# An mLSTM cell and a mixture of depths on one core: output gates loaded and used later, the routed layers one step later

## The chip, the cores and the metric

The kernel runs on one core of a Trainium2 chip. The metric is the device time of one execution in microseconds. A profiled execution also gives a span, from the first to the last instruction of the program; the time lies a little above the span.

Five engines work beside each other, each through its own list of instructions in order: TensorE (PE), VectorE (DVE), ScalarE (ACT), GpSimd (POOL) and SyncE (SP). SP only issues transfers here. All transfers run on the core's 16 DMA engines.

## The reference

Two blocks follow each other. The first is an mLSTM cell for 4 batches, 8 heads, 768 positions and a head dimension of 40:

```
m_new  = maximum(f[t] + m, i[t]);  f_stab = exp(f[t] + m - m_new);  i_stab = exp(i[t] - m_new)
C = f_stab * C + i_stab * outer(v[t], k[t])
n = f_stab * n + i_stab * k[t]
y[t] = sigmoid(o[t]) * (C @ q[t]) / maximum(abs(n @ q[t]), 1)
```

Its result, with the heads side by side, is x of 4 x 768 rows of 320 numbers. The second block works on each batch of x:

```
scores = x[b] @ w_gate
top_idx = the 128 rows of x[b] with the highest scores
out[b] = x[b];  out[b, top_idx] += sigmoid(scores[top_idx]) * (relu(x[b, top_idx] @ w1) @ w2)
```

w1 is 320 x 1024, w2 is 1024 x 320. Everything is float32.

## The kernel before, in words

**Steps.** The work is cut into 12 steps n = 0 to 11: batch b = n // 3, positions 256 (n % 3) to 256 (n % 3) + 255. A step handles all 8 heads, in chunks of 64 positions. The order of all instructions is written out by hand: each engine runs its instructions in the order in which the program text issues them, and a wait holds all that is behind it on the same engine.

**Loads.** SP issues them. `load(n)` brings v, k and q of a step (320 KB each, in two halves for v and k), `load_o(n)` the output gates o (320 KB, two halves). The table `queue` says at which step's text a load is issued; since SP does little else, only its order in SP's list counts, and the buffer it fills: `k_t`, `q_t`, `v_t` and `o_t` have four buffers each, so `load(n)` must wait until step n - 4's data has been used, and `load_o(n)` until `sigmoid(n - 4)` has run.

**One ordinary step n.** PE makes the scores (`scores`, L300), DVE masks them (`masked`, L306). PE turns the next step's k (`turn` with "kT", L232, ACT copies the result, L234), ACT spreads out the next step's q (`widen`, L216), PE makes the next step's update of the state (`update`, L267, from k and the weighed values wv), and DVE adds it up (`states`, L279 to L287). PE reads the states for this step (`read`, L322), turns the next q ("qT", L232), and adds the part inside the chunks (`attend`, L332). DVE divides (`divide`, L341 to L346), which gives y. POOL weighs the values of step n + 2 (`weigh`, L244). ACT makes the sigmoid of the output gates (`sigmoid`, four instructions, L250), POOL multiplies y by it into x (`output`, L354) and issues the two transfers that store x (`store`, L361). DVE makes the scores of the router from x (`router`, L369). `fill` (L221) issues matmuls whose result nobody reads; the third argument of `turn` counts them.

**The routed block of a batch b.** Once all six groups of 128 scores of a batch are there, `spread` (L405) puts them across all partitions through PE and ACT (L412), `ranks` counts for each row how many are greater, half on DVE (L418), half by signs on ACT (L423), and `select` (L472) makes a table of the chosen. `numbers` (L517) turns it into row numbers. `fetch` (L523) is an indirect transfer on POOL that gathers the chosen rows from the output in DRAM, so it comes behind the stores of that batch; `fetched` (L533, L535) turns them, `layer1` (L560 to L566) and `layer2` (L576) are the two layers, `weighed` (L585) scales the result, and `add` (L589) is an indirect transfer on POOL that adds it to the output in DRAM. The program orders an `add` behind earlier transfers that read or write the same range of output rows, and the other way round; POOL stands until those have landed.

**Where these stand.** Batch 0: spread in step 3, ranks in step 4, fetch in step 6. Step 8 is not an ordinary step: the function `layers(8)` replaces it after its scores. It holds the layers of batches 0 and 1, the outputs of steps 6, 7 and 8 (which steps 6 and 7 leave out), the two adds, and the preparation of step 9. Batch 1's spread stands in step 7, its ranks inside `layers`. Batch 2: spread and ranks at the end of `layers`, numbers and fetch in step 9, layers in step 11. Batch 3 comes at the end.

**PSUM.** The pool `ps_u` has one buffer of two banks, which `update`, the first half of `layer1` and others take in turn; `ps_s` (scores, spread) and `ps_h` (read) have one, `ps_t` (turn and smaller tiles) two.

Of the kernel before, what the change touches and what calls it, by code (L numbers as in the profile page):

```python
# [9 lines left out]
FP = mybir.dt.float32  # L10
# [16 lines left out]
def _fast(ctx, tc, q, k, v, i_gate, f_gate, o_gate, w_gate, w1_in, w2_in, out):  # L27
# [6 lines left out]
    NS = S // 256  # L34
    N = B * NS
# [10 lines left out]
    ps_u = ctx.enter_context(tc.tile_pool(name="ps_u", bufs=1, space=PSUM))  # L46
# [55 lines left out]
    load_kv(0, v_t, v)  # L102
    load(1)
    wg = const.tile([128, DM], FP, name="wg")
    load_o(0)
    load(2)
    load_o(1)
    ident = const.tile([128, 128], FP, name="ident")

    def zero(t):  # L110
# [136 lines left out]
    def sigmoid(n):  # L247
        for r in range(2):
            for c in range(2):
                ACT.activation(out=so_t[n % 3][64 * c:64 * c + 64, r], in_=o_t[n % NO][64 * r:64 * r + 64, c], func=AF.Sigmoid)  # L250
# [98 lines left out]
    def output(n):  # L349
        b, s = divmod(n, NS)  # L350
        for r in range(2):
            x, o = x_t[b % 2][:, 2 * s + r, 0:DM], so_t[n % 3][:, r].rearrange("s h d -> s (h d)")
            order = "s (p j d) -> s j p d"
            POOL.tensor_tensor(out=x.rearrange(order, j=2, d=D), in0=pending[n]["y"][:, r].rearrange("s (j p) d -> s j p d", j=2),  # L354
                               in1=o.rearrange(order, j=2, d=D), op=OP.mult)

    def store(n):
        b, s = divmod(n, NS)
        for c in range(2):
            a = 256 * s + 128 * c  # L360
            (POOL if n < N - 1 else SP).dma_start(out=out[b, a:a + 128, :].rearrange("(r t) d -> t r d", t=64),  # L361
                          in_=x_t[b % 2][64 * c:64 * c + 64, 2 * s:2 * s + 2, 0:DM])

    def router(n):
        b, s = divmod(n, NS)
        x = x_t[b % 2][:, 2 * s:2 * s + 2]
        scr = work.tile([128, DM], FP, name="scr", bufs=1)
        for r in range(2):
            DVE.tensor_tensor_reduce(out=scr, in0=x[:, r, 0:DM], in1=wg, scale=1.0, scalar=0.0,  # L369
                                     op0=OP.mult, op1=OP.add, accum_out=x[:, r, DM:DM + 1])  # L370
        del pending[n]
# [18 lines left out]
    dep = {}  # L390
# [6 lines left out]
    def spread(b, r0, r1, pool=None, copied=True):  # L397

        x, w = x_t[b % 2], r1 - r0
        if pool is None:  # L400
            pB = ps_s.tile([128, 2, 512], FP, name="pB", tag="s")
        else:
            pB = pool.tile([128, 2, 512], FP, name="pB", tag="h")
        for r in range(w):
            PE.transpose(pB[:, r // 4, 128 * (r % 4):128 * (r % 4) + 128],  # L405
                         x[:, r0 + r, DM:DM + 1].to_broadcast([128, 128]), ident)
        return spread_copy(pB, w) if copied else pB

    def spread_copy(pB, w):
        flat = pB.rearrange("p j t -> p (j t)")[:, 0:128 * w]  # L410
        sb = mod.tile([128, 128 * w], FP, name=f"sb{w}", bufs=1)
        ACT.copy(out=sb, in_=flat)  # L412
        return sb
# [206 lines left out]
    def weights2():  # L620
        for h in range(2):
            SP.dma_start(out=w2[:, 4 * h:4 * h + 4], in_=w2_in[512 * h:512 * h + 512].rearrange("(f p) d -> p f d", p=128))

    queue = {0: (load, 3, load_o, 2), 1: (load, 4, load_o, 3, load, 5, load_o, 4), 2: (load, 6, load_o, 5),
             4: (load, 7, load, 8, weights1, None, load_o, 6), 5: (load_o, 7, weights2, None, load_o, 8), 6: (load, 9),
             7: (load, 10), 9: (load_o, 9, load_o, 10, load, 11, load_o, 11)}

    def layers(n):

        fetched(0)  # L630
        read(n)
        ranks(1)
        select(1)
        attend(n)
        layer1(0, 0)
        numbers(1, ps_t.tile([128, 3], FP, name="pi", tag="t"))
        fetch(1)
        sigmoid(n - 2)
        output(n - 2)
        store(n - 2)  # L640
        layer1(0, 4)
        divide(n)
        valued(0)
        sigmoid(n - 1)
        output(n - 1)
        store(n - 1)
        layer2(0)
        router(n - 2)
        router(n - 1)
        fetched(1)  # L650
        weighed(0)
        sigmoid(n)
        output(n)
        store(n)
        valued(1)
        layer1(1, 0)
        router(n)
        layer1(1, 4)
        weigh(n + 1)
        add(0)  # L660
        turn(n + 1, "kT")
        widen(n + 1)
        pB = spread(2, 0, 2 * NS, ps_h, False)
        turn(n + 1, "qT")
        dep[2] = {"sb": spread_copy(pB, 2 * NS)}
        ranks(2)
        layer2(1)
        weighed(1)
        select(2)
        weigh(n + 2)  # L670
        update(n + 1)
        states(n + 1)
        add(1)

    for n in range(N):
        b, s = divmod(n, NS)
        more = n + 1 < N
        todo = queue.get(n, ())
        for act, i in zip(todo[0::2], todo[1::2]):
            act(*(() if i is None else (i,)))  # L680
        scores(n)
        masked(n)
        if n == 8:
            layers(n)
            continue
        if n == 0:
            update(0)
            states(0)
        if n in (3, 6, 11):
            router(n - 1)  # L690
        if n == 4:
            ranks(0)
            select(0)
        if more:
            turn(n + 1, "kT", (0, 2, 6, 2, 2, 4)[n] if n < 6 else 0)
            widen(n + 1)
        if 0 < n and more:
            update(n + 1)
            if n != 9:
                states(n + 1)  # L700
            if n not in (3, 6, 7, 9):
                router(n - 1)
        if not more:
            sigmoid(n)
            gated(n)
            fill(ps_t.tile([128, 128], FP, name="pf", tag="t"), 2)
        read(n)
        if n == 9:
            numbers(2, ps_s.tile([128, 2, 512], FP, name="pi", tag="s")[:, 0, 0:3])
            states(n + 1)  # L710
        if n + 2 < N and n != 7:
            weigh(n + 2)
        if n == 6:
            fetch(0)
        if n == 0:
            update(1)
            states(1)
        if more:
            turn(n + 1, "qT")
            if n in (3, 7):  # L720
                dep[n // 4] = {"sb": spread(n // 4, 0, 2 * NS)}
            if n not in (6, 7):
                sigmoid(n)
        else:
            fetched(b - 1, 2)
            dep[b] = {"sb4": spread(b, 0, 4)}
            layer1(b - 1, 0)
            valued(b - 1)
            ranks_first(b)
        attend(n)  # L730
        divide(n)
        if n == 4:
            numbers(0, spare(n + 1)[:, 1, 0:3])
        if n == 9:
            fetch(2)
        if more and n not in (6, 7):
            output(n)
            store(n)
        if n == 0:
            POOL.memset(k_t[3][:, :, :, D:DP], 0.0)  # L740
            tables()
        if n == 1:
            margins()
# [376 lines left out]
```

## Time and profile before

| what | value |
|---|---|
| time, median of 3 runs | 163.75 us (161.92 to 165.38) |
| the profiled execution: time | 163.37 us |
| the profiled execution: span | 161.3 us |
| granted TensorE clock, mean | 0.989 |
| busy: PE, DVE, ACT, POOL | 144.5, 95.2, 89.0, 84.5 us |
| moved by DMA | 24.31 MB, of which 18.75 MB through SP's queue and 4.92 MB through POOL's |

How to read it: a matmul in float32 shows as two records on PE, and weight loads (PEld) overlap matmuls. In the lists below a row has the start and the length in microseconds, the engine ("q" after it: its queue, which issues transfers), the line of the kernel, the operation, what it writes and reads, the shape and the count; in brackets stands how long the engine was idle before it, and what ended that. A row of a group (it begins with the line) ends with the busy time, the mean nanoseconds of one instruction, and the idle time before. A row of transfers ends with the kilobytes of one, if they are known, and the median microseconds from issue to landing. A row with three numbers between strokes gives the shortest, the median and the longest instruction in nanoseconds.

### The profile page before, as it was taken

To read this page: it belongs to the slowest core of one execution; us is meant where nothing else is said; L and a number is where in the kernel's file an instruction comes from. 1 tells how busy PE (TensorE), PEld (TensorE's weight loads), DVE (VectorE), ACT (ScalarE), POOL (GpSimd) and SP (SyncE) were. 2 spreads that over 40 slices of the span, in tenths; PEclk is the share of its full clock that TensorE was granted. 3 is DMA by queue.
4 is the path that set the end of the run, shared out by engine and by line. 5 is a ranking of instruction groups with operands and counts; after the bars stand their busy time and mean duration, and the time that the engine had idled before them with its cause. 6 is when DMAs were issued, how large, how long until landed. Compare 5 with 4: busy or idle time off the path is not lost.

```text
span 161.3 us, 6676 instructions
## 1 busy us (share of the span) xinstructions
PE 144.5 (90%) x2864; PEld 125.4 (78%) x2864; DVE 95.2 (59%) x251; ACT 89.0 (55%) x179; POOL 84.5 (52%) x114
## 2 busy tenths in 40 slices
PE   7989899998998998899989989799999999999900
PEld 7779789997987987799878779579888897898500
DVE  6478384656769957594596542197776959411000
ACT  1667396566598747425475675874648669213000
POOL 7137278988575492892004969847480924212020
PEclk9999999999999999999999999999999999999995
DMA  4999899999979989999989999999513210330110
GB/s 88 198 163 196 137 169 205 188 186 205 194 169 227 187 161 208 175 262 296 157 240 232 206 266 172 216 190 184 100 45 87 46 39 4 81 41 0 53 51 2
DMA packets 91880, 24.31 MB, mean 151 GB/s; under 512 B 88097, under 2 KB 90466, under 8 KB 91842
## 3 DMA queue, kind: packets, MB, share of 16 engines
q1 hardware_dynamic: 89920, 18.75, 65.1%
q0 software_dynamic: 1728, 4.92, 11.0%
q8 instruction: 24, 0.39, 1.1%
q10 hardware_dynamic: 194, 0.13, 0.3%
q14 instruction: 14, 0.11, 0.2%
HBM read 19.20 MB, written 4.59 MB: 147 GB/s over the span
## 4 chain that ended last, share of the span: by engine, by line
PE 63%; DMA 14%; ACT 7%; issue 5%; DVE 5%; ACTq 1%; POOL 1%; DVEq 0%; POOLq 0%
PE pt L232 10%; DMA k<-in_k_dram 9%; PE pU L267 9%; PE py L576 8%; PE pH L332 7%; PE pH L322 6%; PE pU L560 6%; PE pS L300 4%; PE ph L560 2%; DMA i_sb<-in_i_gate_dram 2%; PE pU L564 2%; DMA xe<-out_dram,idx 2%; PE pX L498 2%; ACT sgn L423 1%; PE pt L221 1%
## 5 line engine op out<-in xcount | busy, mean ns | idle before, releaser
L244 POOL TENSOR_TENSOR wv<-v,cols 64x656 f32<-64x656 f32 x23 | 30.1, 1312 | 25.0 <-DMA v<-in_v_dram 14.1
L354 POOL TENSOR_TENSOR x<-y,so 128x320 f32<-128x320 f32 x24 | 21.1, 896 | 10.9 <-DVE y L346 4.2
L236 ACT COPY qT<-pt 128x512 f32<-128x512 f32 x24 | 13.8, 635 | 17.2 <-PE pt L232 17.2
L250 ACT ACTIVATE so<-o 64x320 f32<-64x320 f32 x48 | 22.4, 467 | 0.9
L234 ACT COPY kT<-pt 128x512 f32<-128x512 f32 x24 | 13.3, 587 | 15.0 <-PE pt L232 15.0
L369 DVE CUSTOM_DVE_ANT_0 scr<-x,wg 128x320 f32<-128x320 f32 x22 | 13.8, 628 | 8.1 <-POOL x L354 6.5
L576 PE MATMUL py<-w,hT 128*128 128x320 f32 x64 | 18.2, 437 | 0.3 <-ACT qT L236 0.3
L279 DVE TENSOR_TENSOR C<-pU,C 128x164 f32<-128x164 f32 x40 | 13.1, 327 | 7.0 <-PE pU L267 5.9
L267 PE MATMUL pU<-wv,k 128*64 128x82 f32 x384 | 16.5, 237 | 0.7 <-issue 0.7
L267 PEld LDWEIGHTS pU<-wv,k 128*64 128x64 f32 x384 | 14.5, 137 | 2.8 <-issue 2.2
L332 PE MATMUL pH<-wv,P 128*64 128x82 f32 x384 | 16.3, 237 | 0.0
L576 PEld LDWEIGHTS py<-w,hT 128*128 128x128 f32 x64 | 11.8, 190 | 5.1 <-ACT qT L236 0.5
L332 PEld LDWEIGHTS pH<-wv,P 128*64 128x64 f32 x384 | 14.4, 136 | 1.8 <-issue 1.0
L232 PE MATMUL pt<-ident,k 128*128 128x128 f32 x96 | 13.7, 279 | 2.3 <-DMA k<-in_k_dram 2.1
L361 POOL DMA_DIRECT2D out_dram<-x x22 | 13.9, 635 | 3.3 <-POOL x L354 3.3
L418 DVE TENSOR_SCALAR_CACHE_REDUCE cmp<-sb,x 128x768 f32<-128x768 f32 (+2 forms) x14 | 12.0, 857 | 6.0 <-ACT sb L412 5.7
L300 PE MATMUL pS<-qT,kT 40*64 40x64 f32 x768 | 14.8, 221 | 0.8 <-issue 0.5
L306 DVE TENSOR_TENSOR P<-pS,mask 128x1024 f32<-128x1024 f32 x12 | 14.6, 1214 | 0.6 <-PE pS L300 0.6
L523 POOL DMA_INDIRECT xe<-out_dram,idx x4 | 4.3, 1086 | 19.9 <-DVE den L341 13.8
L322 PE MATMUL pH<-C,qT 40*64 40x41 f32 x704 | 14.0, 229 | 0.8 <-issue 0.6
L300 PEld LDWEIGHTS pS<-qT,kT 40*64 40x64 f32 x768 | 12.8, 134 | 2.3 <-issue 0.7
L232 PE MATMUL pt<-ident,qw 128*128 128x128 f32 x96 | 13.1, 279 | 1.4 <-ACT qw L216 1.4
(141 smaller groups left out, 229.6 us busy)
## 6 DMA issues: line engine op xcount, KB each, us to landing
k<-in_k_dram SPq DMA_DIRECT2D x24, 160.0 KB, 5.0
q<-in_q_dram SPq DMA_DIRECT2D x12, 320.0 KB, 5.4
v<-in_v_dram SPq DMA_DIRECT2D x24, 160.0 KB, 4.8
o<-in_o_gate_dram SPq DMA_DIRECT2D x24, 160.0 KB, 5.0
out_dram<-x POOLq DMA_DIRECT2D x22, 160.0 KB, 4.4
w<-in_moe_w_dram SPq DMA_DIRECT2D x2, 640.0 KB, 5.8
w<-in_moe_w_dram SPq DMA_DIRECT2D x2, 512.0 KB, 6.0
out_dram<-x SPq DMA_DIRECT2D x2, 160.0 KB, 2.6
```

Source lines behind the costliest of these rows:

```text
L232: PE.transpose(pt[:, p, :], src[:, c, 2 * p:2 * p + 2, :].rearrange("s j d -> s (j d)"), ident)
L236: ACT.copy(out=T.rearrange("e p (u t) -> e t p u", t=2)[:, c], in_=pt)
L244: (DVE if n == 0 and r else POOL).tensor_tensor(out=wv_t[n % 3][o, :, :, r], in0=v_t[n % NB][o], op=OP.mult, in1=cols[s][o, 0:2, b * H:b * ...
L250: ACT.activation(out=so_t[n % 3][64 * c:64 * c + 64, r], in_=o_t[n % NO][64 * r:64 * r + 64, c], func=AF.Sigmoid)
L267: PE.matmul(pU[64 * j:64 * j + 64, c, p], k_t[n % NB][:, c, 2 * p + j, :], wv_t[n % 3][:, c, 2 * p + j], start=True, stop=True)
L300: PE.matmul(pS[o, j, c, p, :], kT[e, p, t], qT[e, p, t], start=True, stop=True)
L306: DVE.tensor_tensor(out=P.rearrange(flat), in0=pending[n].pop("pS").rearrange(flat), op=OP.mult, in1=mask.unsqueeze(1).to_broadcast([128, ...
L322: PE.matmul(g["pH"][64 * c:64 * c + 64, NP * j + p, r], g["qT"][e, p, t], state[n, 2 * c + r][e, p, :], start=(c, j) not in g["begun"], st ...
L332: PE.matmul(g["pH"][64 * c:64 * c + 64, NP * j + p], g["P"][:, j, c, p, :], wv_t[n % 3][:, c, 2 * p + j], start=(c, j) not in g["begun"], ...
L354: POOL.tensor_tensor(out=x.rearrange(order, j=2, d=D), in0=pending[n]["y"][:, r].rearrange("s (j p) d -> s j p d", j=2), in1=o.rearrange(o ...
L361: (POOL if n < N - 1 else SP).dma_start(out=out[b, a:a + 128, :].rearrange("(r t) d -> t r d", t=64), in_=x_t[b % 2][64 * c:64 * c + 64, 2 ...
L576: PE.matmul(d["py"], hT_t[:, f, half(b)], w2[:, f, :], start=(f == 0), stop=(f == NF - 1))
```

## The change

It moves work between steps and adds none; four fills go.

- **Loads.** In SP's order o(0) comes behind load(2), o(1) to o(5) come one to three loads later, and load(9) goes ahead of the weights and of o(6) to o(8). o(9) comes ahead of load(10), where it stood behind it.
- **Outputs.** The tables `made` and `scored` say in which step the sigmoid, output and router of which step are issued: output 0 in step 0, 1 in step 2, 2 in step 3, 3 in step 5, 4 and 5 in step 7; 6 to 9 inside `layers`; 10 in step 10.
- **Stores.** Those of steps 0 to 2 are issued together in step 6, those of steps 3 to 5 together in step 7.
- **Batch 0.** Spread in step 4, ranks and select in step 5, fetch in step 7.
- **Layers.** `layers(9)` replaces step 9 instead of step 8. Batch 1's spread moves into it, and takes `ps_u`. Step 9's own output, with its sigmoid and store, stands inside it, between batch 2's spread and its ranks; `add(1)` leaves it.
- **Batch 2.** numbers, fetch and then `add(1)` in step 10; its layers stay in step 11.

```diff
     load(1)
     wg = const.tile([128, DM], FP, name="wg")
+    load(2)
     load_o(0)
-    load(2)
-    load_o(1)
...
-        if pool is None:
+        if pool is ps_u:
+            pB = ps_u.tile([128, 2, 512], FP, name="pU")
+        elif pool is None:
...
-    queue = {0: (load, 3, load_o, 2), 1: (load, 4, load_o, 3, load, 5, load_o, 4), 2: (load, 6, load_o, 5),
-             4: (load, 7, load, 8, weights1, None, load_o, 6), 5: (load_o, 7, weights2, None, load_o, 8), 6: (load, 9),
-             7: (load, 10), 9: (load_o, 9, load_o, 10, load, 11, load_o, 11)}
+    queue = {0: (load, 3, load_o, 1), 1: (load, 4, load_o, 2, load, 5), 2: (load, 6, load_o, 3), 3: (load, 7),
+             4: (load, 8, load_o, 4, load_o, 5), 5: (load, 9, weights1, None, load_o, 6),
+             6: (load_o, 7, weights2, None), 8: (load_o, 8, load_o, 9, load, 10), 10: (load_o, 10, load, 11, load_o, 11)}
+    made = {0: (0,), 2: (1,), 3: (2,), 5: (3,), 7: (4, 5), 10: (10,)}
+    scored = {1: (0,), 3: (1,), 4: (2,), 6: (3,), 8: (4, 5), 10: (9,)}
...
         read(n)
+        dep[1] = {"sb": spread(1, 0, 2 * NS, ps_u)}
         ranks(1)
...
         dep[2] = {"sb": spread_copy(pB, 2 * NS)}
+        sigmoid(9)
+        output(9)
+        store(9)
         ranks(2)
...
         states(n + 1)
-        add(1)
...
-        if n == 8:
+        if n == 9:
             layers(n)
...
-            turn(n + 1, "kT", (0, 2, 6, 2, 2, 4)[n] if n < 6 else 0)
+            turn(n + 1, "kT", (0, 2, 4, 2, 2, 2)[n] if n < 6 else 0)
...
-            if n not in (3, 6, 7, 9):
-                router(n - 1)
+            for i in scored.get(n, ()):
+                router(i)
...
-        if n == 9:
+        if n == 10:
             numbers(2, ps_s.tile([128, 2, 512], FP, name="pi", tag="s")[:, 0, 0:3])
             states(n + 1)
-        if n + 2 < N and n != 7:
+            fetch(2)
+            add(1)
+        if n < 8:
             weigh(n + 2)
         if n == 6:
+            for i in range(3):
+                store(i)
+        if n == 7:
             fetch(0)
...
-            if n in (3, 7):
-                dep[n // 4] = {"sb": spread(n // 4, 0, 2 * NS)}
-            if n not in (6, 7):
-                sigmoid(n)
+            if n == 4:
+                dep[0] = {"sb": spread(0, 0, 2 * NS)}
+            for i in made.get(n, ()):
+                sigmoid(i)
...
-        if n == 9:
-            fetch(2)
-        if more and n not in (6, 7):
-            output(n)
-            store(n)
+        for i in made.get(n, ()):
+            output(i)
+            if n > 8:
+                store(i)
+        if n == 7:
+            for i in range(3, 6):
+                store(i)
```

More of the change, by code (lines that the diff above doesn't have):

```diff
@@ L637, in layers @@
         fetch(1)
-        sigmoid(n - 2)
-        output(n - 2)
-        store(n - 2)
+        sigmoid(6)
+        output(6)
+        store(6)
         layer1(0, 4)
@@ L643, in layers @@
         valued(0)
-        sigmoid(n - 1)
-        output(n - 1)
-        store(n - 1)
+        sigmoid(7)
+        output(7)
+        store(7)
         layer2(0)
-        router(n - 2)
-        router(n - 1)
+        router(6)
+        router(7)
         fetched(1)
         weighed(0)
-        sigmoid(n)
-        output(n)
-        store(n)
+        sigmoid(8)
+        output(8)
+        store(8)
         valued(1)
         layer1(1, 0)
-        router(n)
+        router(8)
         layer1(1, 4)
@@ L688, in _fast @@
             states(0)
-        if n in (3, 6, 11):
+        if n == 11:
             router(n - 1)
-        if n == 4:
+        if n == 5:
             ranks(0)
@@ L698, in _fast @@
             update(n + 1)
-            if n != 9:
+            if n != 10:
                 states(n + 1)
-            if n not in (3, 6, 7, 9):
-                router(n - 1)
+            for i in scored.get(n, ()):
+                router(i)
         if not more:
@@ L719, in _fast @@
             turn(n + 1, "qT")
-            if n in (3, 7):
-                dep[n // 4] = {"sb": spread(n // 4, 0, 2 * NS)}
-            if n not in (6, 7):
-                sigmoid(n)
+            if n == 4:
+                dep[0] = {"sb": spread(0, 0, 2 * NS)}
+            for i in made.get(n, ()):
+                sigmoid(i)
         else:
@@ L731, in _fast @@
         divide(n)
-        if n == 4:
+        if n == 5:
             numbers(0, spare(n + 1)[:, 1, 0:3])
-        if n == 9:
-            fetch(2)
-        if more and n not in (6, 7):
-            output(n)
-            store(n)
+        for i in made.get(n, ()):
[5 more added lines that the diff above has]
+                store(i)
         if n == 0:
```

## The prediction

> **What bounds the kernel now.** I read the page first, then the windows, then TensorE's timeline, then the queues of SyncE (SP) and GpSimd (POOL).
>
> ```profile
> span 161.3 us, 6676 instructions
> PE 144.5 (90%) x2864; PEld 125.4 (78%) x2864; DVE 95.2 (59%) x251; ACT 89.0 (55%) x179; POOL 84.5 (52%) x114
> DMA  4999899999979989999989999999513210330110
> q0 software_dynamic: 1728, 4.92, 11.0%
> q<-in_q_dram SPq DMA_DIRECT2D x12, 320.0 KB, 5.4
> xe<-out_dram,idx POOLq DMA_INDIRECT x4, 3.2
> ```
>
> The row below is from the windows: length, busy time and count of PE, PEld, DVE, ACT and POOL, granted clock, share of the 16 DMA engines, GB/s.
>
> ```profile
> 3.00:116.00 113.00, 106.38 (x2320) 92.54 (x2323) 73.72 (x187) 70.95 (x135) 67.68 (x83) 1.00 1.03 198
> ```
>
> Two things are full at once. PE is busy 90% of the span, and from 3 to 116 us the DMA engines are full too (share 1.03; the page's digits fall to 5 and below after that). So until 116 us a transfer lands when the work queued ahead of it is done, and only its place in the queue counts. TensorE's timeline shows where steps begin (their scores, L300) and where PE waits:
>
> ```profile
> 28.71 1.16 PE L300 MATMUL pS<-qT,kT 40*64 40x64 f32 x64
> 37.97 0.71 PE L221 MATMUL pt<-hot 128*128 128x128 f32 x4
> 64.52 0.63 PE L232 MATMUL pt<-ident,k 128*128 128x128 f32 x4 [0.66 <-DMA k<-in_k_dram]
> 70.80 1.16 PE L300 MATMUL pS<-qT,kT 40*64 40x64 f32 x64
> 76.20 0.82 PE L405 MATMUL pB<-ident,x 128*128 128x128 f32 x6
> 78.24 1.16 PE L300 MATMUL pS<-qT,kT 40*64 40x64 f32 x64
> 81.94 1.36 PE L332 MATMUL pH<-wv,P 128*64 128x82 f32 x32
> 85.86 0.31 PE L517 MATMUL pi<-place,sel 128*128 128x3 bf16 x6
> 99.25 1.09 PE L232 MATMUL pt<-ident,k 128*128 128x128 f32 x8
> 101.69 1.09 PE L232 MATMUL pt<-ident,qw 128*128 128x128 f32 x8 [0.70 <-ACT qw L216]
> 108.84 1.16 PE L300 MATMUL pS<-qT,kT 40*64 40x64 f32 x64
> 110.95 1.35 PE L267 MATMUL pU<-wv,k 128*64 128x82 f32 x32
> 115.76 1.15 PE L300 MATMUL pS<-qT,kT 40*64 40x64 f32 x60
> 123.16 1.16 PE L300 MATMUL pS<-qT,kT 40*64 40x64 f32 x64
> 127.73 0.32 PE L405 MATMUL pB<-ident,x 128*128 128x128 f32 x1 [0.32 <-DVE x L369]
> ```
>
> Step 7 (70.80 to 78.24) takes 7.44 us and waits for nothing; 0.66 of it is the spread (0.82 less the 0.16 by which neighbouring groups overlap), so a bare step is 6.78. Steps 2 to 6 (28.71 to 70.80) take 8.42 on average: fills, and waits for k. Up to step 7 the loads set the pace; from `layers` (78.24 to 108.84 with step 8 around it) PE does.
>
> **The change part by part.** (1) *Loads.* The SP queue gives the price of a transfer in the full stretch:
>
> ```profile
> 31.22 1.74 SPq L65 DMA_DIRECT2D v<-in_v_dram  x2
> 39.69 1.83 SPq L65 DMA_DIRECT2D v<-in_v_dram  x2
> 63.17 2.77 SPq L65 DMA_DIRECT2D v<-in_v_dram  x2
> 67.90 0.64 SPq L69 DMA_DIRECT2D q<-in_q_dram  x1
> 68.59 2.35 SPq L615 DMA_DIRECT2D w<-in_moe_w_dram  x1
> 98.28 0.57 SPq L69 DMA_DIRECT2D q<-in_q_dram  x1
> ```
>
> From 63.17 to 68.59 one bare load (v, k, q) goes out: 5.4 us. From 31.22 to 39.69 it is a load, one output gate o and a step's stores: 8.5. q0 carries 22 stores and 8 indirect transfers in 11.0% of 161.3 = 17.7 us: 0.6 each, 1.2 for a step's two. So a gate costs 8.5 - 5.4 - 1.2 = 1.9. Ahead of loads 3 to 8 the new queue has 1, 1, 1, 2, 2 and 2 gates fewer, and no stores: they land 2 us (load 3) to 8 us (load 7) sooner. PE, not DMA, then paces steps 2 to 7.
>
> (2) *Fills.* A pair is 0.55 (0.71 less the overlap). Four fills go, and with k early the ones left stand on PE's path: step 1 ends at 28.71 as before, step 2 takes 6.78 + 1.10, steps 3 to 5 take 6.78 + 0.55 each, with the spread (0.66) in step 4 and `numbers` (0.24) in step 5, steps 6 and 7 are bare. Step 8 starts at 28.71 + 7.88 + 7.33 + 7.99 + 7.57 + 13.56 = 73.0 instead of 78.24: 5.2 us gained. One doubt: o(0) now goes behind load(2), and `sigmoid(0)` stands ahead of step 1's kT copies on ACT. That costs 0 to 0.5; I take 0, since those copies are due only at the next scores.
>
> (3) *Step 8 is an ordinary step now and needs v(9), k(9), q(9).* q(8) landed at 67.90 + 5.4 = 73.3. Ahead of it two or three steps' stores (2.4 to 3.6) have gone to later places; behind it comes load(9), 5.4: q(9) lands near 75.7, k(9) 1.8 sooner (q is a third of a load), v(9) 3.6 sooner, 72.1. PE is at kT(9) at 74.1 and its second half at 74.7: no wait to speak of. On POOL the wv of `weigh(9)` stands until v(9) is there and takes 2.65 (row below): 74.8. Behind it queue `fetch(0)`, output(4), output(5) and six stores; output(5) ends near 79.5, and its router holds `divide(8)` on DVE for about half a us. Two sigmoids at the end of step 7 (8 x 0.467 = 3.7) make step 8's widen some 0.6 late. Step 9 starts at 80.4. fetch(0) goes out near 75 and lands in 3.2, against a need at 81.5; twice that would still do.
>
> (4) *`layers` one step later.*
>
> ```profile
> 69.39 2.65 POOL L244 TENSOR_TENSOR wv<-v,cols 64x656 f32<-64x656 f32 x2
> 67.39 0.72 ACT L216 COPY qw<-q 128x640 f32<-128x640 f32 x1 [0.55 <-DMA q<-in_q_dram]
> 103.38 0.81 ACT L412 COPY sb<-pB 128x768 f32<-128x768 f32 x1
> L250 ACT ACTIVATE so<-o 64x320 f32<-64x320 f32 x48 | 22.4, 467 | 0.9
> 107.41 1.00 DVE L433 TENSOR_SCALAR cnt<-cnt 128x3 f32<-128x3 f32 x1
> 108.44 0.96 DVE L472 TENSOR_TENSOR sel<-iota,cnt 128x768 bf16<-128x768 f32 x1
> 109.67 1.05 DVE L279 TENSOR_TENSOR C<-pU,C 128x164 f32<-128x164 f32 x3
> ```
>
> `spread(1)` moves into it (0.66 on PE), and ranks(1) and select(1) come behind it. From the copy of a spread to its sel took 103.38 to 109.40, 6.0 us, of which L433 is 1.00; without that 5.2. PE has attend and layer1 in between, 81.94 to 85.86, 3.9: it waits 1.3 to 2.1 at `numbers(1)`; I take 1.3. From scores to `numbers` it was 7.6 and is 9.6; from there to kT 13.4 as before: PE is at kT(10) at 80.4 + 9.6 + 13.4 = 103.4. There it meets load(10), which stands behind o(8) and o(9). Before, q(10) landed at 98.28 + 5.4 = 103.7 behind o(0) to o(8), the weights and the same stores; now one gate more is ahead: 105.6, k(10) at 103.8. So the end of `layers` waits for q(10), and PE's losses since step 8 are hidden under it. widen is 0.72, and from qT (101.69) to the next scores (108.84) it is 7.15 as before: 105.6 + 0.1 + 0.72 + 7.15 = 113.6 for the scores of step 10. Before, step 9 was at 108.84: 4.8 behind, with one step fewer to go (115.76 to 123.16, 7.4). That leaves 2.6 us ahead.
>
> (5) *`sigmoid(9)` inside `layers`* stands on ACT ahead of the signs of ranks(2): 4 x 0.467 = 1.9. select(2) and, behind it on DVE, the states that empty pU come as much later. Before, pU was free at 109.67 + 1.05 = 110.72 and update(10) began at 110.95. So update(11) waits 0.9 (if L433 is short) to 1.7; I take 1.3.
>
> (6) *`fetch(2)` and `add(1)` move to step 10, ahead of output(10) on POOL.*
>
> ```profile
> 114.03 0.16 DVE L482 SCALAR_TENSOR_TENSOR idx<-pi,off 128x1 int32<-128x1 f32 x1
> 114.86 1.29 POOL L244 TENSOR_TENSOR wv<-v,cols 64x656 f32<-64x656 f32 x1 [2.62 <-DMA out_dram<-yg,idx]
> 124.97 1.70 POOL L354 TENSOR_TENSOR x<-y,so 128x320 f32<-128x320 f32 x2 [3.74 <-DVE y L346]
> L589 POOL DMA_INDIRECT out_dram<-yg,idx x4 | 6.3, 1587 | 10.1 <-DVE yg L583 5.3 <-ACT yg L585 4.0 <-POOL wv L244 0.9
> L361 POOL DMA_DIRECT2D out_dram<-x x22: 592/628/823, 25.0 to 127.6; - x22
> ```
>
> The second row shows POOL standing until an add has landed, ahead of the next indirect transfer on the same output rows. add(1) writes rows out of the range that fetch(2) reads, so I expect it to stand until fetch(2) has landed, with output(10) behind it. Counted from the step's scores: idx 5.35 (114.03 + 0.16 - 108.84), fetch issued 5.6, landed 8.8, add (1.59) from 9.1 to 10.7, output(10) (1.70) to 12.4. Before it ended at 124.97 + 1.70 - 115.76 = 10.9. Its router feeds the spread of 127.73, for which PE already waits 0.32: 1.5 us on the path. If the add does not wait, it is done by 8.6, before y(10) is there, and the cost is 0; I take 1.5.
>
> What follows is unchanged. **Sum** on the profiled execution: -2.6 + 1.3 + 1.5 = +0.2, a span of 161.5. That execution took 163.37 (2.07 beside its span), so 163.6; the median of the runs shown, 163.75, is 0.4 above that execution.
>
> [...]
>
> **The rivals.** *A, the new waits don't come* (faster). Without the waits of parts 5 and 6 the end is 2.8 sooner, 160.8; if load(10) is there as well when PE asks, and PE doesn't wait for `numbers(1)` and widen (1.9 less, kT(10) at 101.5), step 10 starts at 101.5 + 2.44 (99.25 to 101.69) + 7.15 = 111.1, 2.5 sooner than in my sum: 158.3. The middle of the two, 159.6, is what I count as A. For it: none of the waits of parts 4 to 6 stands in this trace. Against: the share of 1.03 leaves load(10) nothing to catch up with.
> *B, the load queue slips* (slower). PE stands in `layers` for q(10), so from 105.6 on each us of lateness there goes to the end one to one: at 109.5 it is 167.5, past 2%. For it: the twelve held stores come in bursts among loads made of far smaller pieces, and the weights, wanted in `layers`, stand ahead too. Against: the work is the same, and the engines ran full until 116 whatever lay in the queues.
> *C, the change doesn't do what it says*: steps 2 to 7 stay at 8.4 although k is early, because ACT, DVE or POOL sets them. Step 9 starts near 85, PE is at kT(10) at 108 and at step 10's scores at 117.6, four us past my 113.6: 167.6. Against it stands step 7.
> *D, POOL's stores stand still*: at their longest here six are 1.2 us longer than at the median, and `weigh(9)`, waiting for v(9) anyway, covers that. From 8 us on they would make step 8 late, and past 10 the end.
>
> **How the numbers follow.** About 2% (3.3 us) is what a measurement of this kernel can tell from no change. The forecast, 163.6 and 161 to 166.5 around it, has 0.52; A 0.20; B 0.17; C 0.09; D 0.02. Faster by over 2% is A, 0.20; slower is B, C and D, 0.28; within 2% is the forecast, 0.52. The range goes from A, 159.6, to B, 167.5.
>
> **What would show it.** Right: step 8's scores near 73.0; PE waiting for k(10) or its qw at the end of `layers`; step 10's scores near 113.6; about 1 us of PE idle ahead of update(11); POOL idle about 2 us before the add of step 10, and PE waiting over 1 us for L369 ahead of layer1 in step 11. Wrong: step 8 near 78 (C); q(10) landed before 103 or after 109 (A, B); the add of step 10 issued right behind its fetch. A gain of under 4 us at step 8 would break the first half of the sum, no wait for load(10) the second.

## The result, and the profile after

The changed kernel takes 178.89 us (median of 4 runs, 178.12 to 180.87), the kernel before 164.15 in the same series (161.92 to 165.38): a ratio of 1.097, with a 95% interval of 1.081 to 1.114. It is slower by some 10%, far outside the range. The profiled execution took 180.87 us with a span of 178.8; the spans of the others were 1.7 to 2.8 us shorter. Executions of one kernel fall into faster and slower ones: medians and ranges here are of all runs, ratios of the faster runs alone. One thing in the change lies under the largest loss: `weigh(11)` stands in `layers(9)`, `load(11)` only in the queue of step 10, behind it. So in this kernel step 11 weighs the values of step 7, which are still in that buffer (not what the reference asks), and the load has to wait until they have been read.

The page of the kernel after, the same rows as before; PEclk is the granted clock in tenths:

```profile
span 178.8 us, 6653 instructions
PE 150.6 (84%) x2856; PEld 131.0 (73%) x2856; DVE 95.9 (54%) x251; ACT 88.7 (50%) x179; POOL 85.4 (48%) x114
PEclk9999999999999999999996999997569969999995
DMA  4999999999987999899996993143951230220110
```

PE's share fell from 90% to 84% though its busy time rose by 6.1 us: it waits, and then runs at a lower clock (a mean of 0.939, 0.989 before). The steps that answer to the rows of before, in TensorE's timeline (start, length, line, shape; in brackets the idle time before and what ended it):

```profile
62.36 0.29 PE L518 MATMUL pU<-place,sel 128*128 128x3 bf16 x6 [1.50 <-DVE C L278]
78.21 1.41 PE L299 MATMUL pS<-qT,kT 40*64 40x64 f32 x64
85.49 0.81 PE L299 MATMUL pS<-qT,kT 40*64 40x64 f32 x40
94.30 0.49 PE L561 MATMUL pU<-xeT,w 128*128 128x128 f32 x2 [1.64 <-issue]
95.53 3.66 PE L561 MATMUL ph<-xeT,w 128*128 128x128 f32 x16
112.83 1.09 PE L231 MATMUL pt<-ident,qw 128*128 128x128 f32 x8 [0.69 <-ACT qw L215]
119.98 1.16 PE L299 MATMUL pS<-qT,kT 40*64 40x64 f32 x64
128.38 2.13 PE L231 MATMUL pt<-ident,k 128*128 128x128 f32 x8 [7.25 <-DMA k<-in_k_dram]
130.45 2.46 PE L266 MATMUL pU<-wv,k 128*64 128x82 f32 x32
136.48 1.16 PE L299 MATMUL pS<-qT,kT 40*64 40x64 f32 x64
143.36 0.48 PE L406 MATMUL pB<-ident,x 128*128 128x128 f32 x1 [2.75 <-DVE x L368]
144.27 3.15 PE L561 MATMUL pU<-xeT,w 128*128 128x128 f32 x16
```

The scores (L299) cut the span into stages. Set against what the prediction's sum has for each (its span was 161.5):

| stage | before | predicted | after | after less predicted |
|---|---|---|---|---|
| start to step 8 | 78.24 | 73.0 | 78.21 | +5.2 |
| step 8, now an ordinary step | - | 7.4 | 7.28 | -0.1 |
| `layers` | 30.60 | 33.2 | 34.49 | +1.3 |
| the ordinary steps behind `layers` | 14.32 (two) | 8.2 (one) | 16.50 (one) | +8.3 |
| step 11 to the end | 38.1 | 39.6 | 42.3 | +2.7 |

The last column adds up, but for rounding, to 17.3, the whole miss of the span. In the fourth stage PE stands 7.25 us for k(11). SP's queue and its waits show why:

```profile
102.34 2.93 SPq L75 DMA_DIRECT2D o<-in_o_gate_dram  x2
123.20 0.99 SPq L65 DMA_DIRECT2D v<-in_v_dram  x2
SPq L65 <- POOL wv L243: 18.8, 2, 17.8
119.68 3.49 POOL L243 TENSOR_TENSOR wv<-v,cols 64x656 f32<-64x656 f32 x2
```

SP has nothing to issue from 105.3 to 123.20, because `load(11)`, next in its order, waits 17.8 us for POOL's wv. The last row is `weigh(11)`, which ends at 123.2 behind the outputs, stores and the add of `layers`. The load could have gone out at 105.3; k(11) lands only at 128.4. The windows show the second half of that price (length, busy and count of PE, PEld, DVE, ACT and POOL, granted clock, DMA share, GB/s):

```profile
94.00:102.00 8.00, 7.70 (x48) 6.58 (x49) 5.60 (x15) 4.39 (x10) 4.36 (x6) 0.79 0.88 161
120.00:128.00 8.00, 1.14 (x66) 1.00 (x64) 5.24 (x12) 0.73 (x3) 3.09 (x2) 0.68 0.72 113
128.00:136.00 8.00, 7.62 (x140) 6.59 (x142) 1.43 (x7) 2.94 (x6) 0.20 (x1) 0.68 0.56 85
```

In both windows, during the wait and after it, the granted clock has a mean of 0.68: the turn of k takes 2.13 us where it took 1.09, the update 2.46 where it took 1.35. The same happens on a smaller scale after 94.30 (3.66 for 2.03) and after 143.36 (3.15).

### The profile page after: what moved, and what is told of

It reads as the page before. It is cut to its first block, busy times and chain, and to the rows that moved or that the text cites. A ratio compares the mean times of both kernels' runs of the same rounds, so it can differ in the third digit from the quotient of the medians.

```text
span 178.8 us, 6653 instructions
## 1 busy us (share of the span) xinstructions
PE 150.6 (84%) x2856; PEld 131.0 (73%) x2856; DVE 95.9 (54%) x251; ACT 88.7 (50%) x179; POOL 85.4 (48%) x114
## 5 line engine op out<-in xcount | busy, mean ns | idle before, releaser
L243 POOL TENSOR_TENSOR wv<-v,cols 64x656 f32<-64x656 f32 x23 | 31.1, 1352 | 29.6 <-DMA v<-in_v_dram 22.1
L353 POOL TENSOR_TENSOR x<-y,so 128x320 f32<-128x320 f32 x24 | 21.6, 909 | 14.1 <-ACT so L249 6.5
L266 PE MATMUL pU<-wv,k 128*64 128x82 f32 x384 | 17.9, 247 | 2.1 <-issue 1.5
L368 DVE CUSTOM_DVE_ANT_0 scr<-x,wg 128x320 f32<-128x320 f32 x22 | 13.3, 603 | 10.6 <-POOL x L353 9.0
L266 PEld LDWEIGHTS pU<-wv,k 128*64 128x64 f32 x384 | 15.6, 144 | 4.6 <-issue 4.5
L231 PEld LDWEIGHTS pt<-ident,k 128*128 128x128 f32 x96 | 11.5, 150 | 8.1 <-issue 7.7
L331 PE MATMUL pH<-wv,P 128*64 128x82 f32 x384 | 16.6, 237 | 0.0
L299 PE MATMUL pS<-qT,kT 40*64 40x64 f32 x768 | 15.0, 222 | 1.3 <-issue 0.9
L331 PEld LDWEIGHTS pH<-wv,P 128*64 128x64 f32 x384 | 14.5, 136 | 2.1 <-issue 1.5
L299 PEld LDWEIGHTS pS<-qT,kT 40*64 40x64 f32 x768 | 13.0, 134 | 2.9 <-issue 1.3
```

The source lines that it names most:

```text
L231: PE.transpose(pt[:, p, :], src[:, c, 2 * p:2 * p + 2, :].rearrange("s j d -> s (j d)"), ident)
L243: (DVE if n == 0 and r else POOL).tensor_tensor(out=wv_t[n % 3][o, :, :, r], in0=v_t[n % NB][o], op=OP.mult, in1=cols[s][o, 0:2, b * H:b * ...
L266: PE.matmul(pU[64 * j:64 * j + 64, c, p], k_t[n % NB][:, c, 2 * p + j, :], wv_t[n % 3][:, c, 2 * p + j], start=True, stop=True)
L299: PE.matmul(pS[o, j, c, p, :], kT[e, p, t], qT[e, p, t], start=True, stop=True)
L331: PE.matmul(g["pH"][64 * c:64 * c + 64, NP * j + p], g["P"][:, j, c, p, :], wv_t[n % 3][:, c, 2 * p + j], start=(c, j) not in g["begun"], ...
```

## The experiments

**e1: `load(11)` back where step 11's values are in time.**

```diff
-  8: (load_o, 8, load_o, 9, load, 10), 10: (load_o, 10, load, 11, load_o, 11)}
+  8: (load_o, 8, load_o, 9, load, 10), 9: (load, 11), 10: (load_o, 10, load_o, 11)}
```

> The changed kernel with load(11) issued at step 9, ahead of weigh(11) in the text, and nothing else moved. Theory (the load of step 11 stands behind weigh(11), which the text puts ahead of it on the same value buffer): PE's wait of 7.25 us for k(11) goes, and with it the low clock behind it (turn and update 2.13 + 2.46 instead of 1.09 + 1.35): 9 us or a little less, so about 170 us. Rival (k(11) would be late anyway, since the DMA engines are full with o(8), o(9), load(10) ahead): a wait of several us stays at the turn of step 10 and the time is 175 or more.

Measured: 170.00 us, ratio to before 1.038 (1.025 to 1.050). TensorE's timeline of e1:

```profile
117.64 1.16 PE L299 MATMUL pS<-qT,kT 40*64 40x64 f32 x64
121.17 1.35 PE L266 MATMUL pU<-wv,k 128*64 128x82 f32 x32 [1.34 <-DVE C L278]
125.98 1.49 PE L299 MATMUL pS<-qT,kT 40*64 40x64 f32 x64
132.94 0.32 PE L406 MATMUL pB<-ident,x 128*128 128x128 f32 x1 [2.24 <-DVE x L368]
```

Step 10 takes 8.34 us instead of 16.50. By the medians the late load is worth 8.9 us of the 14.7. With it gone, the wait of part 5 comes to light: 1.34 us ahead of update(11), predicted 1.3.

**e2: `add(1)` behind output(10) and store(10), nothing else** (moved to the end of step 10; load(11) late as in the change), and **e3: e1 and e2 together.**

> The changed kernel with add(1) behind output(10) and store(10) instead of ahead of them; load(11) stays late. Theory (add(1) stands on POOL until fetch(2) has landed, and output(10) with it): PE's wait of 2.75 us for the router in step 11 falls to 0.3, and layer1 behind it is at full clock (3.15 to 1.95): 3 to 4 us, about 175. Rival (output(10) waits for something else, its sigmoid or y(10)): under 1 us.

> Both edits together. If the two costs are apart, their gains add: 178.9 - 9 - 3.5 = about 166. If the sum of the prediction was right in all the rest, 162.3 (its 163.6 less the 1.3 to 1.5 of the add). The difference between the two is what is lost ahead of step 10: I expect 166, as step 8 began at 78.21 and not at 73.0.

Measured: e2 176.71 us (1.080, 1.069 to 1.091), e3 167.31 (1.023, 1.012 to 1.033). By the medians the add costs 2.2 us beside the late load and 2.7 without it, more than the 1.5 of the prediction and less than the 3 to 4 expected of e2. The rows of POOL in e1 show the mechanism as predicted: the add waits until fetch(2) has landed, and output(10) waits behind it:

```profile
125.30 1.11 POOL L524 DMA_INDIRECT xe<-out_dram,idx  x1 [4.46 <-PE pt L231]
129.13 1.66 POOL L590 DMA_INDIRECT out_dram<-yg,idx  x1 [2.72 <-DMA xe<-out_dram,idx]
130.86 1.67 POOL L353 TENSOR_TENSOR x<-y,so 128x320 f32<-128x320 f32 x2
```

e3 is the change without its two accidents, and still 2.3% slower than before. Its stages: step 8 at 76.71 (1.5 gained, not 5.2), `layers` 33.17 (+2.6 against before), step 10 8.35, step 11 to the end 38.7. Up to step 8 the kernel after, e1, e2 and e3 run the same text, and step 8 begins at 78.21, 77.34, 77.53 and 76.71: single executions differ by 1.5 us there, so 3.7 of the 5.2 us that the table shows as lost are lost in all four.

**e4: e3 without the fills** (all fill counts of the turns 0).

> Both edits, and no fills in steps 1 to 5. If PE sets the pace of steps 1 to 5, the 12 fills of 0.27 us go from the path: 3.3 us less than with both edits. If a chain through DVE and ACT sets it (spread, ranks, numbers of batch 0), the fills only pass the time of a wait and at most 1 us is gained; PE then waits longer for L368, for the states or for qw.

Measured: 165.66 us (1.010, 1.001 to 1.020), 1.65 less than e3. Half of the fills' 3.3 us comes back; part of the rest stands in longer waits (in front of numbers(0) 1.76 us instead of 1.26). What fills are worth is taken up again below.

**e5: the kernel before with nearly the change's load order, and nothing else** (load(2) ahead of o(0), gates one to three loads later, load(9) ahead of the weights).

> The kernel before with nothing changed but the order of the loads: k, v and q go early and the output gates late, as the change orders them; outputs, routers, stores and the layers stay where they were. If loads set the pace of steps 2 to 7, as my prediction had it, step 8 begins at about 73 us (before 78.2) and the time is about 159. If the chain of VectorE and ScalarE around the routers and the ranks sets it, as the profile after seems to show, the waits for k go and others take their place: step 8 at 76.5 to 78, time 162 to 165.

Measured: 176.60 us (1.069, 1.057 to 1.080): neither of the two. An output that is still made in its own step needs its gate there. ScalarE and TensorE in step 4:

```profile
54.27 1.93 ACT L249 ACTIVATE so<-o 64x320 f32<-64x320 f32 x4 [6.99 <-DMA o<-in_o_gate_dram]
61.01 1.97 PE L231 MATMUL pt<-ident,qw 128*128 128x128 f32 x8 [8.31 <-ACT qw L215]
```

The sigmoid stands 6.99 us for its gate, and the widening of the next q, behind it on ACT, holds PE for 8.31. So later outputs are what makes later gates possible; but the run does not say what the early loads are worth by themselves.

**e6: e3 with numbers(0) on a PSUM buffer of the turns.** **e7: e3 with every store right behind its output.**

> e3 with one thing moved: the PSUM tile of batch 0's numbers comes from the buffers of the turns and no longer from the tile of the updates, so TensorE need not wait there until VectorE has emptied that tile (1.26 us in e3, 1.50 after the change). If that wait was a true part of the lost gain, the time is 1 to 1.3 us lower, about 166.2, and step 6 begins 1.2 us earlier. If the selection itself is late (the same VectorE queue), TensorE waits at the same place for the selection instead, and the time stays at 167.3.

> e3 with the stores no longer held: each store follows its output on POOL's queue, as before the change. If the held stores, let go in two bundles, cost something (the 1.64 us in which TensorE waits for its next instructions at step 9 falls while the second bundle is in flight), that wait falls below 0.8 us and the time is about 166. If holding them pays, because loads and stores no longer share the queues in steps 1 to 5, steps 2 to 5 get longer and the time is 168 to 169. If neither, 167.3 within 0.8.

Measured: 167.64 us (1.021, 1.012 to 1.031) and 167.43 (1.021, 1.010 to 1.033): both as e3. Holding the stores is worth nothing either way; the wait at step 9 that the expectation names is 1.46 us in e7 and 1.64 in e3. In e6 the wait in front of numbers(0) is gone, and another has come:

```profile
60.17 0.31 PE L518 MATMUL pi<-place,sel 128*128 128x3 bf16 x6
63.76 1.08 PE L231 MATMUL pt<-ident,k 128*128 128x128 f32 x4 [1.34 <-issue]
64.77 2.27 PE L266 MATMUL pU<-wv,k 128*64 128x82 f32 x32
64.00:68.00 4.00, 4.00 (x84) 3.55 (x83) 1.63 (x4) 1.31 (x2) 4.00 (x6) 0.66 0.87 167
```

PE, ahead by the wait that went, stands 1.34 us at "issue", where the profile shows nothing that it waits for. The expectations and this text read that as a wait for its own instructions, which is an inference (the last section has what speaks for it). The clock falls to a mean of 0.66 in 4 us (last row, a window), and step 6 takes 9.94 us instead of 7.01.

**e8: sigmoid(9), output(9), store(9) behind ranks(2).**

> e3 with sigmoid(9), output(9) and store(9) behind ranks(2) and no longer ahead of them. My prediction's part 5 says that the ranks wait for the four activations of sigmoid(9) and the update of step 11 then waits 1.3 us for VectorE; e3 shows 1.34 us there. So that wait falls to below 0.4 us and the time is about 166.1. If VectorE is late for a reason of its own, the wait stays above 1 us and the time at 167.3; if output(9) now comes late for its router, step 10 or 11 waits instead, with 167 to 168.

Measured: 173.59 us (1.057, 1.038 to 1.075), a clear miss. POOL, then PE:

```profile
117.91 1.83 POOL L353 TENSOR_TENSOR x<-y,so 128x320 f32<-128x320 f32 x2 [4.15 <-ACT so L249]
121.33 2.82 POOL L243 TENSOR_TENSOR wv<-v,cols 64x656 f32<-64x656 f32 x2
124.20 1.55 PE L266 MATMUL pU<-wv,k 128*64 128x82 f32 x32 [3.59 <-POOL wv L243]
```

VectorE is early now, but output(9) comes 4.0 us later on POOL than in e3, weigh(11) stands behind it, and update(11) waits 3.59 us for that instead of 1.34 for VectorE. Step 10 takes 13.58 us instead of 8.35, more than the wait: the clock fell here too (the 32 matmuls of L331 behind it take 2.46 us, 1.36 in e3). Both orders can be had at once only with output(9) earlier, which e9 and e12 do.

**e9 and e12: `layers` in the order that e3, e4 and e8 point to**, without the fills (e9) and with them (e12), on e3.

```diff
+        dep[1] = {"sb": spread(1, 0, 2 * NS, ps_u)}
         read(n)
-        dep[1] = {"sb": spread(1, 0, 2 * NS, ps_u)}
...
         layer1(1, 0)
+        sigmoid(9)
         router(8)
+        output(9)
         layer1(1, 4)
...
-        sigmoid(9)
-        output(9)
-        store(9)
         ranks(2)
...
         weigh(n + 2)
+        store(9)
         update(n + 1)
```

> e3 without the fills of the turns (as e4) and with two things placed by what e4 shows. The spread of batch 1 stands ahead of read(9) in the layers and not behind it: TensorE waits 1.07 us there for y of step 8, and the ranks begin some 2 us earlier, so that the 1.35 us wait for the selection of batch 1 goes too. And sigmoid(9) and output(9) stand behind the first half of the first layer of batch 1, where ScalarE is idle for 1.90 us and POOL for about 1 us, with the store behind weigh(11): so neither the ranks (1.34 us at the update of step 11) nor the weighing (3.59 us in e8) waits for them. If these waits are real costs, the time is 165.7 - 0.9 - 1.35 - 1.3 = about 162.2, under the time before. If instruction supply or the clock takes them back, as after e6, it stays at 164.5 to 166.

> e9 with the fills of the turns kept: 16 matmuls more in steps 1 to 5 that do nothing but keep TensorE busy. e4 against e3 gained 1.65 us by leaving them out, about half of their 3.3 us. If the same holds here, the time is 1.6 us above that of e9, about 163.8; if the fills keep the clock up where waits fall in steps 4 to 6 (granted clock 0.73 and 0.85 in e4 against 1.00 in e3 between 60 and 68 us), it is the same as e9's.

Measured: e9 164.80 us over 11 runs, from 162.27 to 169.75, with a ratio of 0.993 (0.987 to 0.999), some 163 us and so between the two times expected. e12 166.01 over 4 runs, from 164.10 to 167.91: too scattered for a ratio. The step behind `layers` takes 6.93 us in e12 instead of 8.35, and nothing waits ahead of update(11). (The fills kept are 12, not the 16 of the expectation.)

**e10: e3 without spread and ranks of batch 0.** **e11: e3 without two thirds of the gates.**

> e3 without the spread and the ranks of batch 0: a constant table stands in for them, so that the first 128 tokens are selected (that part of the computation is left out); selection, numbers, fetch and layers stay. If the chain of routers, spread and ranks on VectorE and ScalarE took the early gain, as I now think, the 0.8 us of waits and 0.9 us of work in the spread of step 4 and the 1.26 us in front of numbers(0) go: step 8 begins at 73.7 (76.7 in e3, 73.0 predicted) and the time is about 164.3. If transfers are the bound underneath, waits for k or for TensorE's own instructions take their place: step 8 at 75.5 or later, time above 166.

> e3 without the loads of the output gates of steps 4 to 11, two thirds of the 640 KB a step with the short 160-byte rows (these steps use the gates of steps 0 to 3): less for the 16 DMA engines, the same work on all others. If the waits in which TensorE waits for its own instructions (0.97, 0.68, 0.66, 0.47 and 1.64 us in e3) come from DMA engines that are full, they go: step 8 at about 74 and the time about 163.5. If they belong to TensorE's sequencer or to the program's size, they stay: time 166.5 to 167.3.

Measured: e10 166.70 us (1.013, 1.007 to 1.019), e11 170.12 (1.038, 1.031 to 1.046). In e10 both theories turn out to be right, one behind the other:

```profile
74.51 1.16 PE L299 MATMUL pS<-qT,kT 40*64 40x64 f32 x64 [0.36 <-ACT so L249]
76.94 0.63 PE L231 MATMUL pt<-ident,k 128*128 128x128 f32 x4 [1.27 <-DMA k<-in_k_dram]
85.42 0.56 PE L299 MATMUL pS<-qT,kT 40*64 40x64 f32 x19 [1.22 <-issue]
84.00:92.00 8.00, 6.00 (x109) 5.14 (x102) 4.32 (x12) 2.06 (x5) 2.92 (x5) 0.65 1.03 277
```

Without that chain step 8 begins at 74.51, 2.2 us sooner than in e3. Then PE waits for k(9), then for instructions, and the clock has a mean of 0.65 from 84 to 92 us; at step 10 (118.90) e10 is 1.3 us behind e3. e11 told nothing of full engines: a step's gates are 320 KB, not the 640 of the expectation, the loads that were left moved up, the DMA engines stayed full (share 1.07 from 60 to 90 us), and a wait for instructions of 2.63 us at step 8 is the longest of all runs on e3.

**e13: e3 without the loads of steps 6 to 11**, which does empty the engines.

> e3 without the loads of k, v, q and the output gates of steps 6 to 11 (those steps compute with what the buffers hold from steps 2 to 5; that part of the computation is changed); the weights and the stores still go. The DMA engines should be far below full from about 55 us on. If the waits of TensorE for its own instructions (0.66, 0.47 and 1.64 us at steps 8 and 9 in e3) come from full DMA engines, they fall below 0.2 us each and the time is about 164.5 (167.3 less 2.8). If they are TensorE's sequencer, they stay and the time is 167 or a little less. Neither theory expects the waits in the spread (0.8 us), in front of numbers(0) (1.26 us) and at the update of step 11 (1.34 us) to change.

Measured: 166.21 us (1.018, 1.002 to 1.034; from 164.64 to 170.06). The window of e13, then that of e3, then a row of e13:

```profile
60.00:95.00 35.00, 31.11 (x816) 27.80 (x817) 25.00 (x70) 20.56 (x41) 19.91 (x25) 1.00 0.25 69
60.00:95.00 35.00, 30.79 (x833) 27.40 (x832) 25.65 (x65) 19.98 (x40) 19.10 (x24) 1.00 1.03 240
92.65 0.31 PE L522 MATMUL pi<-place,sel 128*128 128x3 bf16 x6 [1.35 <-DVE sel L477]
```

With a DMA share of 0.25 in place of 1.03 the waits of 0.66, 0.47 and 1.64 us at steps 8 and 9 are gone; the longest left after 60 us is 0.41. So the long ones come from DMA engines that are full. But 1.35 us of the 1.64 come back at once as a wait for the selection of batch 1, which had been hidden under it. The two profiled executions are 2.0 us apart (spans of 162.6 and 164.6), not the 2.8 that had been expected; the runs of e13 scatter too much to say more of the time.

**e14: e12 with numbers(0) as in e6.**

> e12 (layers in the mended order, fills kept) with numbers(0) on a PSUM buffer of the turns, as in e6. The 1.02 us that TensorE waits in front of numbers(0) in e12 goes. If it is a cost of its own, the time is about 165.0 (e12 166.0); if TensorE, ahead by that much, then waits for its own instructions or for k instead, as in e6 and e10, it stays at 166.

Measured: 163.99 us over 12 runs, ratio 1.000 (0.995 to 1.005). The mended change is as fast as the kernel before, no faster: its spans are equal (161.3 us both). PE still waits 1.70 us for instructions at 63.90, but the clock stays up in the profiled execution (1.00 from 20 to 120 us).

**e15: e14 without fills. e16: the kernel before without fills.**

> e14 (layers in the mended order, numbers(0) on a buffer of the turns) without the fills. If the fills are a cost of their own, half of their 3.3 us comes back, as in e4: about 162.3, under the time before. If they only fill time in which TensorE would wait for VectorE, k or its own instructions, or keep its clock up, the time stays at 164.

> The kernel before without its 32 fill matmuls in steps 1 to 5 (16 pairs of turns, 0.18 us each by the profile). In the kernel before these steps are followed by waits for k (0.39, 0.27, 1.10 us), so if the loads set the pace there, the waits grow by what the fills leave: 164 within 0.8. If TensorE sets the pace, the time is some 1.5 us lower, about 162.7.

Measured: 167.60 us (1.008, 0.998 to 1.017; from 164.51 to 172.97) and 169.62 (from 164.57 to 172.21, too scattered for a ratio), beside 165.11 for the kernel before. In neither run does leaving out the fills gain time. Whether it costs time these runs don't show: e15 is not told apart from before, and the shortest run of e16 lies among those of the kernel before. The clock does differ: all twelve runs have a lower mean granted clock (0.925 to 0.968) than all eleven of the kernel before (0.971 to 0.989). Two waits of TensorE and two windows of e16, and last the fills that stand in the kernel before at the first of the two places:

```profile
31.57 0.79 PE L232 MATMUL pt<-ident,k 128*128 128x128 f32 x4 [1.60 <-DMA k<-in_k_dram]
87.47 1.93 PE L332 MATMUL pH<-wv,P 128*64 128x82 f32 x25 [2.86 <-issue]
28.00:36.00 8.00, 6.40 (x178) 5.50 (x172) 3.66 (x9) 3.45 (x7) 6.61 (x14) 0.79 0.99 190
84.00:92.00 8.00, 5.14 (x57) 4.76 (x50) 4.03 (x9) 2.84 (x6) 0.00 (x0) 0.66 0.89 203
29.80 1.60 PE L221 MATMUL pt<-hot 128*128 128x128 f32 x12
```

Around the wait for k at 31.57 the clock is 0.79 in the mean, around the one for instructions at 87.47 it is 0.66; in the kernel before it stays at 1.00 from 3 to 116 us, and 1.60 us of fills stand there where e16 waits 1.60 us for k. There the fills are not idle work: they bridge a wait. e4's gain of 1.65 us stands against that as a rule, though its clock fell too after numbers(0) (0.73 from 60 to 64 us); no run here says why the gain was left over there.

## Why the prediction was wrong

**The step that failed first: part 4, load(11).** The prediction followed load(10) through `layers` and took what comes behind as "unchanged". It never set the new place of load(11) against `weigh(11)`, which shares its buffer and stands in `layers(9)`. Both stood in the text that it had. Cost by the medians: 8.9 us (e1), of which 7.25 - 1.34 = 5.9 is wait and the rest mostly clock (turn and update took 2.13 + 2.46 us for 1.09 + 1.35). None of the rivals held it; B looked for lateness in the queue's volume, not in a buffer.

**Part 1 and 2, the early gain of 5.2 us.** The loads did come early: between steps 1 and 8 PE waits for no k in the kernel after. But "PE, not DMA, then paces steps 2 to 7" was wrong: these steps take 8.2 us in the mean after and 8.0 in e3, where the sum had 7.4. Rival C, given 0.09 and with 8.4, is what happened to much of this part: VectorE paces steps 4 and 5. Its timeline after:

```profile
60.02 0.96 DVE L473 TENSOR_TENSOR sel<-iota,cnt 128x768 bf16<-128x768 f32 x1
60.90 0.32 DVE L282 COPY C<-pU 128x164 f32<-128x164 f32 x1
```

The states of step 6 are taken out of pU only after ranks and selection, and numbers(0), in the same bank, waits 1.50 us for them (62.36 above); the prediction costed numbers at 0.24 and looked at no wait. "Against it stands step 7" was a poor reason, since step 7 has no ranks. e10 shows 2.2 us for this chain; the 1.5 us that e10's step 8 is still behind 73.0 are traced to no single cause, and after it the waits for k(9) and for instructions take the gain back. Fills as a cost on PE's path (0.55 a pair) came back by half in e4 and not at all in e15 and e16.

**Part 3** came out in its number (7.28 us, 7.4 predicted) by luck. `weigh(9)` shows when v(9) was there:

```profile
75.70 2.62 POOL L243 TENSOR_TENSOR wv<-v,cols 64x656 f32<-64x656 f32 x2 [6.18 <-DMA v<-in_v_dram]
```

That is 3.6 us after the 72.1 of the prediction. In e10, where step 8 begins at 74.51, PE waits 1.27 and 0.35 us for k(9), which the prediction had there at 73.9; after the change the late step 8 hid it. **Part 4's sum for `layers`**, 33.2 us, came near the 34.49 for wrong reasons: PE did not wait for q(10) (0.69 us for qw at 112.83, as the 0.70 before), but asked for k(10) only at 110.39 instead of 103.4, so the landing was never put to the test. It lost 1.64 us for instructions and then its clock (0.79 from 94 to 102 us); the wait at numbers(1), 1.3 in the sum, is 1.35 in e4 and e13, where no wait for instructions lies over it. **Part 5** held: 1.34 us in e1 and e3, 1.3 predicted, and e8 shows that sigmoid(9) is its cause. **Part 6** had the mechanism right and the size wrong: 2.2 to 2.7 us (after to e2, e1 to e3) instead of 1.5. In e1 fetch(2) starts 0.9 us after its index is ready and the add 3.8 us after that, where the sum had 0.25 and 3.5, and PE's wait for the router is 2.24 us. In the kernel after a slower layer 1 follows a wait of 2.75 (3.15 us against 1.95 in the kernel before).

**Rival A** (no new waits) and **D** (stores that stand still) are out: the stores of POOL took 629 ns in the mean, and e7 without the bundles is equal to e3.

What remains open: e14 ends level with before although the waits for load(11), numbers(0), update(11) and the router behind add(1) are gone, so as far as these runs go the change's own idea is worth about nothing here; whether it would gain with fewer bytes to load was not tried in a kernel that computes all steps.

## What to carry to other kernels

When a load is moved, look up who read its buffer last in the program's order, and where that reader now stands; a load that goes behind a reader inherits the whole queue of the reader's engine (17.8 us here). A wait taken away where DMA engines, VectorE and TensorE are all nearly full (in e3 from 60 to 70 us a DMA share of 1.02, and VectorE busy for 8.29 us and TensorE for 8.73) mostly uncovered the next one here: ask for each what is hidden under it, and expect the sum of single gains to be too high. And price a wait of TensorE above its length when the clock may fall with it: the 7.25 us here came with 10.2 us at half clock.

## What the runs showed of the hardware

**Waits for instructions.** TensorE stood up to 2.86 us at "issue" (e16, 87.47) while the DMA engines were full or nearly so (share 0.89 from 84 to 92 us), and at most 0.41 us after 60 us when they were not (e13, share 0.25 from 60 to 95 us). The page after has this row for a DMA queue of the kind "instruction":

```profile
q8 instruction: 24, 0.39, 0.9%
```

24 packets in 0.39 MB are 16 KB each. That it is these packets which TensorE waits for is the author's inference, not shown: the profile names no cause for "issue". In the traces each of the seven waits at "issue" in TensorE's timeline after ends 1.2 to 1.9 us after a packet of this queue has ended (1.3 at 94.30), and each of the four before 1.4 to 1.5 us after one. It is 1.4 us before 83.72 in e11 and 1.6 before 87.47 in e16; in e6 none fits the wait that ends at 63.76.

**The clock.** The windows of 8 us above mix full and lower clock. In windows of 2 us the fall after 94.30 in the kernel after looks so:

```profile
94.00:96.00 2.00, 1.70 (x18) 1.46 (x19) 1.07 (x3) 0.52 (x2) 0.00 (x0) 0.90 0.76 125
96.00:98.00 2.00, 2.00 (x12) 2.00 (x11) 1.86 (x8) 1.83 (x5) 1.45 (x2) 0.50 0.49 85
98.00:100.00 2.00, 2.00 (x15) 1.73 (x15) 1.86 (x3) 0.11 (x1) 1.70 (x3) 0.75 1.11 237
```

In shorter windows there it is 1.00 from 92.00 to 95.50, 0.58 to 96.00, 0.50 to 99.00 and 1.00 to 104.00. Taken as either full or 0.50, the three rows hold 0.4 + 2.0 + 1.0 = 3.4 us at one half. Estimated in the same way from the windows, it is 3.4 us at the waits of 1.34 us (e6: 0.91 and 0.66, 4 us each) and 1.60 (e16: 0.79 in 8 us), 6.8 at the one of 2.86 (e16: 0.83 and 0.83, 10 us each) and 10.2 at the one of 7.25 (after: 0.68 and 0.68, 8 us each). After 1.64 in e3, 1.70 in e14 and 2.63 in e11 it stayed at 1.00, and after 1.57 and 1.17 in e12 the matmuls kept their lengths (1.36 us for the 32 of L331, 2.03 for the 16 of L561). So length alone does not decide. These falls last 3.4 us, or two or three times that; what sets one off, and what sets its length, no run here shows.
